# Top-k attention with two MLPs on one core: spreading each block's MLP work past the next block's start

## The chip, the core and the metric

One core of one Trainium2 chip runs the whole program in one launch. The core has five engines that run side by side, each through its own list of instructions in order: PE (TensorE, matrix products and transposes), DVE (VectorE), ACT (ScalarE), POOL (GpSimd) and SP (SyncE, which only issues DMAs). They wait for each other through semaphores. The metric is the device time of the launch in microseconds (us); a change of about half a per cent is what a measurement of this kernel can tell from none.

## The reference

```
scores = q @ k.T / sqrt(64)          # 4 batches, 8 heads, 576 tokens
kth    = 32nd largest of each row
attn   = softmax over the scores that are >= kth, the others count as nothing
x      = attn @ v                    # put together to 2304 tokens x 512
h      = relu(x @ w_in);   x = (h * h) @ w_out        # first MLP, 512 -> 2048 -> 512
h      = x @ w2_in; x = max(0.01 h, h) @ w2_out       # second MLP, same sizes
```

The weights come as float64, all else as float32.

## The kernel before

The attention is cut into tiles of 128 score rows, two tiles to a pair, 72 pairs in all. A pair's scores come from PE (L303, evacuated by ACT at L304), its 32 largest values from 8 MAX8 and 6 MATCH_REPLACE8 on DVE (L867, L869), its softmax from ACT (L321, L325) and POOL, then PE transposes it (L339 for the first 512 columns, 8 instructions for a pair, L354 for the last 64) and multiplies it with v (L425 for the first two units, L436 from then on). Every fp32 value on the fast matmul path is split into a high and a low part.

The table `UNITS` gives the order in which (batch, first token, tokens) go through the attention: units of 256, 256, 256, 64, 320, 256, 256, 320 and 320 tokens, each over four head pairs. The finished tokens are collected in that order in six blocks of 512, 256, 384, 512, 256 and 384 (`BLOCKS`). When a block is full, its MLP work can start: layer 0 and layer 1, each in 16 steps of 128 hidden rows (the function `moe`). A step is 12 matmuls for the hidden rows (L619) and 6 to 12 for the accumulation (L656 in layer 0, L658 in layer 1); ACT and POOL (DVE in the last block) make the activation between them (L629 to L639). `moe` is a generator that gives up control after every three matmuls; such a portion is called a quantum below.

Block 0 is special: its 32 steps are the first to use the weights, so 32 times 1 MB of float64 is loaded (L511, `wraw`), turned into high and low parts by ACT, DVE and POOL (L532 to L553, `wc`, `wi`, `wo`) and stored to DRAM (L566, L567) for the later blocks, which load the parts back (L574, L575).

A block's x lies in one of three buffer sets (`SETS` = 0, 1, 0, 1, 0, 2), so block 2 writes where block 0 was, and block 3 where block 1 was. The end of each unit and head pair is `x_out`, which writes x into the block that is being filled.

The order of the program is written by a loop over slots at the end of the function, 16 slots for a pair, one DVE instruction in 14 of them. In each slot, events (scores, transposes, v products, loads) are emitted with a higher priority, and then `run_moe` emits as many quanta as the current rate has earned. The rate of a block was fixed ahead: its quanta over the slots until the next block is full, less one (`rate`). When the next block is full, whatever is left of the one before is emitted at once. From this, a scheduler with a priority for each instruction makes the final list of each engine; attention is put ahead where its inputs are thought to be ready, and MLP matmuls fill in.

By those slots blocks 0 to 5 are full about when the transposes of pairs 16, 24, 36, 52 and 62 and the end of the attention are reached.

The unit of 64 tokens is `KEPT`: its scores are made early, beside batch 0's others, parked in DRAM and loaded back when its turn comes. `HI_SET` (0 to 15) lists which unit-and-head-pair numbers have the high part of q and v made by ACT; for the others POOL makes it.

Of the kernel before, what the change touches and what calls it, by code (L numbers as in the profile page):

```python
# [24 lines left out]


UNITS = [
    (0, 0, 256), (0, 256, 256), (1, 0, 256), (0, 512, 64), (1, 256, 320),
    (2, 0, 256), (3, 0, 256), (2, 256, 320), (3, 256, 320),
]  # L30

# [6 lines left out]
SETS = (0, 1, 0, 1, 0, 2)  # L38
# [5 lines left out]

NATIVE = 2

KEPT = 3

EARLY = (2, 3)
FILL = (2, 245)  # L50
# [13 lines left out]
LEAD = 24  # L64

SOON = 100
SEAM = 400
CONVP = 30

# [17 lines left out]
def topk_attention_moe_moe2_kernel(  # L87
# [97 lines left out]
    for i in range(4):  # L185
        x = const if i < 2 else ahead
# [206 lines left out]
    blocks = []  # L393
# [78 lines left out]
    def unspill(blk):  # L472
        m = blk["spilled"]
        for c, (xh, xl) in enumerate(block_x(blk)):
            split_hi(xh[:, 0:m], spill[:, c, 0:m])
            POOL.tensor_tensor(xl[:, 0:m], spill[:, c, 0:m], xh.bitcast(F)[:, 0:m], op=OP.subtract)
# [201 lines left out]
    def quanta(j, layer):  # L678
        return NF * (NK + (NK if layer == 0 else blocks[j]["n"] // P))
# [121 lines left out]
    for uh in uhs:  # L801
# [16 lines left out]
        if uh["u"]["i"] == NATIVE - 1 and uh["hp"] == NHP - 1:  # L818
            at(z, open_late)
        rmark(uh, z)  # L820
    rate = []
    for j, blk in enumerate(blocks):
        nxt = rslot[j + 1] if j + 1 < len(blocks) else rslot[j] + 40
        rate.append(sum(quanta(*ph) for ph in groups[j]) / max(nxt - rslot[j] - 1, 40))

    def convert_now(i):
        for _ in w_convert(i):
            pass
# [12 lines left out]
    def run_moe(amount):  # L841
        while amount >= 1 and active:
            try:
                next(active[0])
                amount -= 1
            except StopIteration:
                active.pop(0)
        return amount
# [3 lines left out]
    while slot <= last:  # L852
        p, i = divmod(slot, 16)
        if slot >= 0 and p < NPAIRS:
            pr = pairs[p]
            if i == 0:
                pr["m8"] = pool.tile([P, 2, 32], F, tag="m8", name="m8", bufs=2)
                pr["sum"] = pool.tile([P, 2], F, tag="sum", name="sum", bufs=2)
                pr["rc"] = pool.tile([P, 2], F, tag="rc", name="rc", bufs=2)
                for t in pr["t"]:  # L860
                    t["w"] = pool.tile([P, S], F, tag="w", name="w", bufs=2)
            x = i % 2
            t = pr["t"][x]
            m8 = pr["m8"]
            r = i // 4
            if i < 14 and i % 4 < 2:
                cur["dve"] = DVE.max(out=m8[:, x, 8 * r:8 * r + 8], in_=t["s"] if r == 0 else t["w"])  # L867
            elif i < 14:
                cur["dve"] = DVE.match_replace(out=t["w"], in_to_replace=m8[:, x, 8 * r:8 * r + 8],  # L869
                                               in_values=t["s"] if r == 0 else t["w"], imm_value=NEG)  # L870
        if slot == rslot[0]:
            open_mlp()
        for fn, a in events.pop(slot, []):
            nr = len(ready)
            with tc.high_priority(offset=SOON):
                fn(*a)
            for blk in ready[nr:]:
                if not (len(ready) > nr + 1 and blk is ready[-1]):
                    while active:
                        run_moe(1)  # L880
                if blk["idx"] + 1 < len(blocks) and blocks[blk["idx"] + 1].get("spilled"):
                    unspill(blocks[blk["idx"] + 1])
                active.extend(moe(*ph) for ph in groups[blk["idx"]])
                credit = 0.0
                cur["rate"] = rate[blk["idx"]]
        if active:
            credit = run_moe(credit + cur["rate"])
        slot += 1
# [54 lines left out]
```

## Time and profile before

| | us |
|---|---|
| median of the three runs shown (1189.94, 1193.88, 1194.23) | 1193.88 |
| the profiled execution's own time | 1189.77 |
| its span, first to last instruction | 1188.0 |
| PE busy | 1124.0 (95%) |
| DVE busy | 872.1 (73%) |

The rows further down come from the profiled execution. A window row gives the busy time of each engine in a stretch of the span. In the timeline a row merges equal instructions that follow each other; its second number runs to the modelled end of the last one, which overlaps the next row, so the pace of matmuls is read from start to start. An entry in square brackets is idle time just before the row, with what ended it. The chain of waits follows the last instruction of a stretch back to what released each step.

### The profile page before, as it was taken

What the parts mean: (1) busy time and instruction counts of PE and PEld (TensorE: products, weight loads), DVE (VectorE), ACT (ScalarE), POOL (GpSimd) and SP (SyncE); (2) the same over time, 40 slices, a digit from 0 to 9 for tenths busy, and PEclk for the clock granted to TensorE, in tenths of its full rate; (3) what the DMA queues carried; (4) which work ended last, traced back from release to release, by engine and by line L of the source; (5) the groups of instructions that cost most, each with busy time, mean ns of one, the idle gap of its engine ahead of it and who ended that gap; (6) DMA issues with size and microseconds to landing.
All of it is one profiled execution on the core that took longest, in us unless ns stands there. A gap on an engine that the chain in (4) does not pass through costs nothing.

```text
span 1188.0 us, 20096 instructions
## 1 busy us (share of the span) xinstructions
PE 1124.0 (95%) x6376; PEld 985.5 (83%) x6376; DVE 872.1 (73%) x1828; ACT 820.1 (69%) x1823; POOL 744.8 (63%) x958
## 2 busy tenths in 40 slices
PE   5899977989899999999999999999999999999997
PEld 4777765868688899898998998788888899998996
DVE  7999999888886668999999999989997400110010
ACT  6999998899989667887676777556766743332322
POOL 7968846999879677677886775767665653002100
PEclk9999989999899999999999999999999999999999
DMA  9868756899999698799888888667776499779973
GB/s 307 287 216 276 264 187 230 312 334 333 394 353 360 199 336 293 240 346 371 312 264 296 286 283 287 217 219 219 232 234 215 151 326 334 256 252 351 346 258 119
DMA packets 108201, 329.53 MB, mean 277 GB/s; under 512 B 17216, under 2 KB 25408, under 8 KB 104000
## 3 DMA queue, kind: packets, MB, share of 16 engines
q1 hardware_dynamic: 105472, 323.53, 79.8%
q10 hardware_dynamic: 2624, 4.72, 1.1%
q8 instruction: 52, 0.85, 0.3%
q14 instruction: 53, 0.43, 0.1%
HBM read 257.03 MB, written 71.17 MB: 276 GB/s over the span
## 4 chain that ended last, share of the span: by engine, by line
PE 57%; DVE 21%; ACT 12%; DMA 5%; issue 2%; POOL 2%; ACTq 0%; SPq 0%; POOLq 0%; DVEq 0%
PE h L619 22%; PE acc L658 13%; DVE m L867 10%; PE acc L656 9%; DVE w L869 8%; PE att L425 3%; PE att L436 3%; PE att L339 3%; ACT e L321 2%; ACT stage L304 1%; PE sp L303 1%; ACT e L325 1%; DMA wraw<-in_w_dram 1%; DMA out_dram<-y 1%; ACT s L304 1%
## 5 line engine op out<-in xcount | busy, mean ns | idle before, releaser
L619 PE MATMUL h<-xh,wi 128*128 128x512 f32 (+2 forms) x1280 | 345.9, 344 | 9.7 <-ACT ga L629 4.5
L867 DVE MAX8 m<-w 128x8 f32<-128x576 f32 x432 | 315.1, 756 | 1.8
L619 PEld LDWEIGHTS h<-xh,wi 128*128 128x128 f32 x1280 | 225.4, 190 | 38.6 <-ACT ga L629 6.7
L639 POOL TENSOR_TENSOR gl<-ga,gh 128x512 fp32r<-128x512 f32 (+2 forms) x160 | 162.5, 1018 | 137.2 <-ACT gh L638 110.9
L869 DVE MATCH_REPLACE8 w<-m,w 128x576 f32<-128x576 f32 x288 | 215.2, 751 | 0.5
L619 PE MATMUL h<-xl,wi 128*128 128x512 f32 (+2 forms) x640 | 203.3, 338 | 0.0
L347 POOL TENSOR_TENSOR PTs<-whole,PTs 128x512 fp32r<-128x512 f32 x112 | 144.6, 1297 | 43.7 <-ACT whole L346 43.2
L656 PE MATMUL acc<-gh,wo 128*128 128x512 f32 (+2 forms) x768 | 156.5, 343 | 0.8 <-ACT y L674 0.5
L658 PE MATMUL acc<-wo,gh 128*128 128x512 f32 x576 | 152.1, 396 | 0.5 <-ACT gh L638 0.5
L656 PEld LDWEIGHTS acc<-gh,wo 128*128 128x128 f32 x768 | 127.4, 190 | 13.4 <-ACT y L674 0.7
L321 ACT ACTIVATE e<-s,m 128x576 f32<-128x576 f32 x144 | 112.9, 785 | 32.3 <-DVE m L867 27.4
L639 DVE TENSOR_TENSOR gl<-ga,gh 128x384 fp32r<-128x384 f32 x32 | 17.9, 559 | 152.1 <-ACT gh L638 149.4
L619 PEld LDWEIGHTS h<-xl,wi 128*128 128x128 f32 x640 | 120.0, 189 | 10.6
L636 ACT ACTIVATE ga<-h 128x512 f32<-128x512 f32 (+2 forms) x96 | 46.6, 491 | 116.3 <-PE h L619 114.8
L658 PEld LDWEIGHTS acc<-wo,gh 128*128 128x128 f32 x576 | 105.4, 188 | 21.2 <-ACT gh L638 0.9
L867 DVE MAX8 m<-s 128x8 f32<-128x576 f32 x144 | 104.3, 754 | 17.7 <-ACT s L304 15.2
L325 ACT ACTIVATE e<-e,nb 128x576 f32<-128x576 f32 x144 | 111.5, 782 | 1.8 <-POOL nb L315 1.7
L869 DVE MATCH_REPLACE8 w<-m,s 128x576 f32<-128x576 f32 x144 | 108.2, 752 | 0.6
L339 PE MATMUL att<-ident,e 128*128 128x128 f32 x576 | 90.1, 277 | 7.6 <-DVE wc L548 3.0
L334 POOL TENSOR_SCALAR e<-e,rc 128x576 f32<-128x576 f32 x112 | 82.5, 748 | 16.0 <-DVE rc L330 14.5
L656 PE MATMUL acc<-gl,wo 128*128 128x512 f32 (+2 forms) x384 | 88.3, 349 | 3.8 <-POOL gl L639 3.8
L631 POOL TENSOR_TENSOR ga<-ga 128x512 f32<-128x512 f32 (+2 forms) x80 | 66.3, 829 | 36.9 <-ACT gh L630 36.7
(90 smaller groups left out, 2117.4 us busy)
## 6 DMA issues: line engine op xcount, KB each, us to landing
wi<-wd SPq DMA_DIRECT2D x160, 512.0 KB, 5.1
wo<-wd SPq DMA_DIRECT2D x160, 512.0 KB, 5.0
wraw<-in_w_dram SPq DMA_DIRECT2D x32, 1024.0 KB, 7.9
sd<-stage SPq DMA_DIRECT2D x76, 288.0 KB, 3.3
s<-sd SPq DMA_DIRECT2D x76, 288.0 KB, 4.8
wd<-wi SPq DMA_DIRECT2D x32, 512.0 KB, 7.8
wd<-wo SPq DMA_DIRECT2D x32, 512.0 KB, 8.4
vd<-VT SPq DMA_DIRECT2D x16, 640.0 KB, 5.8
```

The source lines that it names most:

```text
L321: ACT.activation(t["e"], t["s"], AF.Prelu, bias=pr["m8"][:, i, 31:32], scale=-1.0, alpha=1.0 / FAR)
L325: ACT.activation(e, e, AF.Exp, bias=pr["nb"][:, i:i + 1], scale=-FAR, accum_out=pr["sum"][:, i:i + 1])
L334: POOL.tensor_scalar(e, e, pr["rc"][:, i:i + 1], 1.0, op0=OP.mult, op1=OP.mult)
L339: PE.transpose(ps[:, j * P:(j + 1) * P], t["e"][:, j * P:(j + 1) * P], ident)
L347: POOL.tensor_tensor(pts[:, 4:8, c:c + P], whole, pts.bitcast(F)[:, 0:4, c:c + P], op=OP.subtract)
L619: PE.matmul(two[r][:, 0:n], lhsT=ws[r][:, w, c * P:(c + 1) * P], rhs=x[c][y][:, 0:n], start=cnt == mine[0], stop=cnt == mine[-1])
L631: POOL.tensor_tensor(a[:, 0:n], a[:, 0:n], a[:, 0:n], op=OP.mult)
L639: (DVE if j >= GLD else POOL).tensor_tensor(gl[:, 0:n], a[:, 0:n], gh.bitcast(F)[:, 0:n], op=OP.subtract)
L656: PE.matmul(acc[c][:, 0:n], lhsT=wo[:, w, cs], rhs=g[:, 0:n], start=first, stop=last)
L658: PE.matmul(acc[c], lhsT=g[:, cs], rhs=wo[:, w, :], start=first, stop=last)
L867: cur["dve"] = DVE.max(out=m8[:, x, 8 * r:8 * r + 8], in_=t["s"] if r == 0 else t["w"])
L869: cur["dve"] = DVE.match_replace(out=t["w"], in_to_replace=m8[:, x, 8 * r:8 * r + 8], in_values=t["s"] if r == 0 else t["w"], imm_value=NEG)
```

## The change

Four things change.

1. A block's quanta are no longer emitted at once when the next block is full. They stay in front of the list, and the next block's are put behind them. The rate is set when a block is full: all quanta then open, over the slots until the next block is full plus 24 (`LATE`). Block 0's rate goes from 256 quanta over 127 slots to 256 over 152.
2. Before an `x_out` opens a new block, everything still open of a block in the same buffer set is emitted.
3. In `UNITS` the 64 tokens of batch 0 go behind the 320 of batch 1, both still in block 2, so that the first `x_out` of block 2 comes after 320 tokens' first head pair and not after 64 tokens'. `KEPT` follows.
4. `HI_SET` is not touched, but its numbers 12 to 15 now mean the head pairs of the unit of 320: their q goes to ACT, and the q and v of the 64 tokens to POOL.

```diff
--- before.py
+++ after.py
@@ -25,7 +25,7 @@
 
 
 UNITS = [
-    (0, 0, 256), (0, 256, 256), (1, 0, 256), (0, 512, 64), (1, 256, 320),
+    (0, 0, 256), (0, 256, 256), (1, 0, 256), (1, 256, 320), (0, 512, 64),
     (2, 0, 256), (3, 0, 256), (2, 256, 320), (3, 256, 320),
 ]
 
@@ -44,7 +44,7 @@
 
 NATIVE = 2
 
-KEPT = 3
+KEPT = 4
 
 EARLY = (2, 3)
 FILL = (2, 245)
@@ -64,6 +64,7 @@
 LEAD = 24
 
 SOON = 100
+LATE = 24
 SEAM = 400
 CONVP = 30
 
@@ -818,11 +819,6 @@
         if uh["u"]["i"] == NATIVE - 1 and uh["hp"] == NHP - 1:
             at(z, open_late)
         rmark(uh, z)
-    rate = []
-    for j, blk in enumerate(blocks):
-        nxt = rslot[j + 1] if j + 1 < len(blocks) else rslot[j] + 40
-        rate.append(sum(quanta(*ph) for ph in groups[j]) / max(nxt - rslot[j] - 1, 40))
-
     def convert_now(i):
         for _ in w_convert(i):
             pass
@@ -841,7 +837,8 @@
     def run_moe(amount):
         while amount >= 1 and active:
             try:
-                next(active[0])
+                next(active[0][0])
+                active[0][1] = max(active[0][1] - 1, 0)
                 amount -= 1
             except StopIteration:
                 active.pop(0)
@@ -872,17 +869,19 @@
             open_mlp()
         for fn, a in events.pop(slot, []):
             nr = len(ready)
+            if fn is x_out and "x" not in blocks[cur["fill"]]:
+                shared = [x for x in range(cur["fill"]) if SETS[x] == SETS[cur["fill"]]]
+                while any(x[2] in shared for x in active):
+                    run_moe(1)
             with tc.high_priority(offset=SOON):
                 fn(*a)
             for blk in ready[nr:]:
-                if not (len(ready) > nr + 1 and blk is ready[-1]):
-                    while active:
-                        run_moe(1)
-                if blk["idx"] + 1 < len(blocks) and blocks[blk["idx"] + 1].get("spilled"):
-                    unspill(blocks[blk["idx"] + 1])
-                active.extend(moe(*ph) for ph in groups[blk["idx"]])
-                credit = 0.0
-                cur["rate"] = rate[blk["idx"]]
+                j = blk["idx"]
+                if j + 1 < len(blocks) and blocks[j + 1].get("spilled"):
+                    unspill(blocks[j + 1])
+                active.extend([moe(*ph), quanta(*ph), ph[0]] for ph in groups[j])
+                todo = sum(x[1] for x in active)
+                cur["rate"] = todo / (rslot[j + 1] - slot + LATE if j + 1 < len(blocks) else 40)
         if active:
             credit = run_moe(credit + cur["rate"])
         slot += 1
```

What this does to PE's list is shown at three places. The number of matmuls of every kind is the same before and after. Line numbers above 66 are one higher in the changed kernel up to the loop (L340 is L339 before, L620 is L619).

The first place is PE's list where block 0 goes from layer 0 to layer 1: `acc` from `gl` and `gh` ends layer 0, `h` from `xh` and `xl` opens layer 1, `att` from `ident` and `e` are the transposes of a pair, `att` from `KT` and `q` are scores. Before:

```order
L656 MATMUL acc<-gh,wo 128x512 x8
L303 MATMUL att<-KT,q_83 128x288
L303 MATMUL att<-KT,q_84 128x288
L339 MATMUL att<-ident,e_107 128x128 x4
L339 MATMUL att<-ident,e_108 128x128 x4
L303 MATMUL att<-KT,q_83 128x288
L303 MATMUL att<-KT,q_84 128x288
L303 MATMUL att<-KT,q_83 128x288
L303 MATMUL att<-KT,q_84 128x288
L656 MATMUL acc<-gl,wo 128x512 x4
L619 MATMUL h<-xh_649,wi 128x512 x4
```

After:

```order
L355 MATMUL att<-ident,e_107 64x128
L355 MATMUL att<-ident,e_108 64x128
L437 MATMUL att<-PTs,VT 128x256 x9
L657 MATMUL acc<-gl,wo 128x512 x4
L657 MATMUL acc<-gh,wo 128x512 x8
L657 MATMUL acc<-gl,wo 128x512 x4
L304 MATMUL att<-KT,q_77 128x288
L304 MATMUL att<-KT,q_78 128x288
L304 MATMUL att<-KT,q_77 128x288
L304 MATMUL att<-KT,q_78 128x288
L620 MATMUL h<-xh_649,wi 128x512 x8
L620 MATMUL h<-xl_650,wi 128x512 x2
```

The eight transposes that stood ahead of the last `gl` accumulation now stand some 30 MLP matmuls earlier, in front of the piece shown; four score matmuls that also stood ahead of it have come behind it.

The second place is PE's list where block 1 begins (`h` of 256 columns is block 1, `acc` from `wo` is still block 0's layer 1). Before:

```order
L339 MATMUL att<-ident,e_107 128x128 x4
L658 MATMUL acc<-wo,gh 128x512 x2
L658 MATMUL acc<-wo,gl 128x512 x4
L619 MATMUL h<-xh_3222,wi 128x256 x4
L619 MATMUL h<-xl_3223,wi 128x256
L658 MATMUL acc<-wo,gh 128x512 x8
L619 MATMUL h<-xh_3222,wi 128x256 x2
L339 MATMUL att<-ident,e_108 128x128
L303 MATMUL att<-KT,q_77 128x288
L339 MATMUL att<-ident,e_108 128x128
L303 MATMUL att<-KT,q_78 128x288
```

After:

```order
L659 MATMUL acc<-wo,gh 128x512
L304 MATMUL att<-KT,q_83 128x288
L304 MATMUL att<-KT,q_84 128x288
L659 MATMUL acc<-wo,gl 128x512 x4
L355 MATMUL att<-ident,e_109 64x128
L355 MATMUL att<-ident,e_110 64x128
L437 MATMUL att<-PTs,VT 128x320
L620 MATMUL h<-xh_3152,wi 128x256 x4
L620 MATMUL h<-xl_3153,wi 128x256
L620 MATMUL h<-xh_3152,wi 128x256 x2
L620 MATMUL h<-xl_3153,wi 128x256
```

Both lists mix the end of block 0 with the opening of block 1. Before, this stands at the transposes of pair 24 (the first and the last rows shown); now it stands behind those of pair 25, with the products with v of the unit of 320 tokens between.

The third place is PE's list at the transposes of pairs 47 and 48 (`h` of 384 columns is block 2, layer 1). Before, from the products with v ahead of pair 48's transposes on:

```order
L619 MATMUL h<-xh_5191,wi 128x384 x4
L658 MATMUL acc<-wo,gh 128x512 x2
L436 MATMUL att<-PTs,VT 128x256 x7
L339 MATMUL att<-ident,e_107 128x128 x2
L436 MATMUL att<-PTs,VT 128x256
L339 MATMUL att<-ident,e_107 128x128 x2
L339 MATMUL att<-ident,e_108 128x128 x4
L658 MATMUL acc<-wo,gh 128x512 x4
L658 MATMUL acc<-wo,gl 128x512 x3
```

After, from pair 47's transposes to pair 48's:

```order
L340 MATMUL att<-ident,e_109 128x128 x4
L340 MATMUL att<-ident,e_110 128x128 x4
L620 MATMUL h<-xl_5297,wi 128x384 x2
L355 MATMUL att<-ident,e_109 64x128
L355 MATMUL att<-ident,e_110 64x128
L437 MATMUL att<-PTs,VT 128x256
L340 MATMUL att<-ident,e_107 128x128 x4
```

Before, 41 MLP matmuls stand between the first transposes of pairs 47 and 48; now there are two.

Counted over the whole list, the MLP matmuls that stand ahead of the first transposes of pair 28, 53 and 71 were 1052, 2184 and 2940, and are 911, 2067 and 2796.

## Rows read from the trace of the kernel before

**Rows 1.** The page, busy time of each engine: time, share, instructions.
```profile
PE 1124.0 (95%) x6376; PEld 985.5 (83%) x6376; DVE 872.1 (73%) x1828; ACT 820.1 (69%) x1823; POOL 744.8 (63%) x958
```

**Rows 2.** Windows: PE, PEld, DVE, ACT, POOL busy, clock, DMA, GB/s.
```profile
178.00:320.00 142.00, 125.64 (x562) 98.38 (x562) 125.63 (x241) 127.69 (x246) 122.59 (x128) 0.95 0.89 316
320.00:450.00 130.00, 129.45 (x747) 112.58 (x748) 91.20 (x181) 101.29 (x207) 97.59 (x109) 1.00 0.89 320
450.00:750.00 300.00, 291.17 (x1836) 270.00 (x1835) 295.68 (x641) 222.96 (x499) 225.08 (x298) 1.00 0.86 294
750.00:950.00 200.00, 199.61 (x990) 166.14 (x989) 167.46 (x362) 132.42 (x276) 130.43 (x157) 1.00 0.66 214
950.00:1188.00 238.00, 229.98 (x1419) 217.66 (x1417) 23.06 (x44) 76.94 (x170) 37.81 (x53) 0.99 0.81 280
```

**Rows 3.** Chain of waits by line: 178:320, 320:450, 450:740.
```profile
by line: DMA wraw<-in_w_dram 11.8%; ACT att L541 7.2%; issue 6.4%; DVE m L867 5.9%; ACT wc L532 5.7%; DVE w L869 5.4%; PE h L619 5.2%; DVE wc L547 5.1%; DVE wc L548 4.4%; PE acc L656 3.9%; ACT wo L552 3.8%; DMA vraw<-in_v_dram 3.7%; PE att 
...
by line: PE h L619 37.3%; PE acc L658 33.7%; PE att L436 6.9%; PE acc L656 6.6%; DMA out_dram<-y 5.5%; PE att L339 3.6%; PE att L303 3.1%; ACT y L674 1.3%; PE att L354 0.7%; ACT s L304 0.4%; ACT PTs L344 0.4%; ACT whole L346 0.4%; issue 0.1
...
by line: DVE m L867 36.3%; DVE w L869 26.8%; PE acc L658 5.6%; PE h L619 5.6%; issue 3.4%; DVE PTs L364 3.0%; DVE xf L442 2.4%; PE att L436 1.8%; ACT e L321 1.6%; DMA out_dram<-y 1.6%; ACT e L325 1.6%; PE att L303 1.5%; ACT PTs L344 1.4%; A
```

**Rows 4.** Timeline of the PE: first transposes of pairs 16, 28, 53 and 71.
```profile
193.18 0.27 PE L339 MATMUL att<-ident,e 128*128 128x128 f32 x1
...
466.51 0.38 PE L339 MATMUL att<-ident,e 128*128 128x128 f32 x2
...
733.76 0.49 PE L339 MATMUL att<-ident,e 128*128 128x128 f32 x3
...
951.27 0.49 PE L339 MATMUL att<-ident,e 128*128 128x128 f32 x3
```

**Rows 5.** Timeline of the PE: back-to-back runs, and the row behind each.
```profile
332.34 2.03 PE L658 MATMUL acc<-wo,gh 128*128 128x512 f32 x8
334.21 0.39 PE L658 MATMUL acc<-wo,gl 128*128 128x512 f32 x1
...
432.94 1.11 PE L656 MATMUL acc<-gh,wo 128*128 128x256 f32 x8
433.90 0.64 PE L656 MATMUL acc<-gl,wo 128*128 128x256 f32 x4
434.37 0.42 PE L303 MATMUL att<-KT,q 128*128 128x288 f32 x2
434.64 0.41 PE L354 MATMUL att<-ident,e 128*64 128x128 f32 x2
...
437.49 1.87 PE L436 MATMUL att<-PTs,VT 128*128 128x64 f32 x16
439.20 0.36 PE L619 MATMUL h<-xh,wi 128*128 128x256 f32 x1
...
694.46 0.33 PE L619 MATMUL h<-xh,wi 128*128 128x384 f32 x1
694.63 0.34 PE L619 MATMUL h<-xl,wi 128*128 128x384 f32 x1
```

**Rows 6.** Windows from pair 16 to pair 28; columns as in rows 2.
```profile
193.00:304.00 111.00, 101.29 (x466) 81.13 (x464) 95.34 (x183) 101.17 (x192) 104.58 (x107) 0.97 0.92 323
304.00:466.00 162.00, 157.04 (x922) 137.01 (x923) 121.92 (x239) 130.47 (x271) 123.58 (x140) 0.98 0.90 324
```

**Rows 7.** Timeline of the PE: its waits where block 0 changes layers.
```profile
304.30 0.66 PE L339 MATMUL att<-ident,e 128*128 128x128 f32 x4 [1.77 <-ACT s L304]
306.53 1.08 PE L339 MATMUL att<-ident,e 128*128 128x128 f32 x4 [1.58 <-DVE wc L548]
```

**Rows 8.** Timeline of the PE: its waits where block 3 begins.
```profile
736.59 0.50 PE L619 MATMUL h<-xh,wi 128*128 128x512 f32 x1 [1.58 <-ACT ga L629]
743.91 1.20 PE L656 MATMUL acc<-gl,wo 128*128 128x512 f32 x4 [1.06 <-POOL gl L639]
```

**Rows 9.** Groups by line, DVE, 320 to 450: count, busy, mean, idle before.
```profile
L547 DVE SCALAR_TENSOR_TENSOR wc<-att,wc 128x512 uint32<-128x512 uint32 x23 | 15.1, 682 | 6.2 <-ACT wc L532 3.8 <-ACT att L541 2.4
```

## The prediction

> **What bounds the kernel now.** I read the page first: PE is busy 95% of the span, DVE 73%, ACT 69%, POOL 63% [rows 1]. That is a mean over unlike stretches, so the windows come next, cut where the busy shares change [rows 2], and beside each the chain of waits [rows 3].
>
> - 178 to 320, the first half of block 0's MLP, with the weight conversion: nobody is full for good. PE has 125.6 of 142 us, ACT 127.7, POOL 122.6, DVE 125.6, and the chain is a mix of weight loads, ACT conversions and DVE. The granted clock averages 0.95: some 14 us at 1.2 GHz.
> - 320 to 450, block 0's second half and the start of block 1: PE has 129.5 of 130 us and the chain is PE's matmuls. DVE is idle for 38.8 us, because the attention comes up late in PE's list.
> - 450 to 750: DVE has 295.7 of 300 us, and MAX8 and MATCH_REPLACE8 are 63% of the chain. PE is at 291.2.
> - 750 to 950: PE again, 199.6 of 200. DVE has 32.5 us idle.
> - From 950 on only MLP work is left, and PE has all of it.
>
> So PE sets the end, except between 450 and 750. The change adds no matmul and takes none away; what it can earn is PE's idle time. Idle after pair 16 begins: about 10 and 5 us between pairs 16 and 28 [rows 6], then 9 us in the DVE stretch [rows 2], and next to nothing in 750 to 950.
>
> **The change part by part.** I divide PE's list at the first transposes of pairs 16, 28, 53 and 71, which started at 193.2, 466.5, 733.8 and 951.3 [rows 4]. The stretches took 273.3, 267.2, 217.5 us, and 236.7 to the end of the span at 1188.0. Prices per matmul come from start-to-start times of unbroken runs [rows 5]: 512 columns (334.21 - 332.34)/8 = 0.23; 384 columns 0.17; 256 columns (433.90 - 432.94)/8 = 0.12; 64 columns (439.20 - 437.49)/16 = 0.107; scores (434.64 - 434.37)/2 = 0.135. Products with v of 320 columns I put at 0.14, between the 256 and 384 columns.
>
> From the two lists, kind by kind:
> - Pair 16 to 28: 141 MLP matmuls of 256 columns fewer (-16.9), the 72 products of the 64 tokens gone (-7.7), 2 of 512 (+0.5), 20 scores and 18 products of 320 tokens more (+5.2). Sum -18.9 us.
> - Pair 28 to 53: those 141 and 72 come in (+24.6), the scores and products go out (-5.2), 48 of 384 (-8.2) and 69 of 512 columns (-15.9) fewer. Sum -4.7 us.
> - Pair 53 to 71: 48 of 384 more (+8.2), 63 of 512 (-14.5) and 12 of 256 (-1.4) fewer. Sum -7.7 us.
> - From pair 71 on: 132 of 512 and 12 of 256 columns more, +31.8 us.
>
> That adds up to nothing, as it must. But a stretch that DVE sets does not get shorter when PE's work in it does. Pair 28 to 53 is 25 pairs at 267.2/25 = 10.7 us, DVE's pace, so its -4.7 us are not earned: **+4.7**. In 53 to 71 DVE would need 18 x 10.7 = 193 us, under PE's 217.5 - 7.7, so PE's saving counts there.
>
> PE's idle time from pair 16 to 28. The work of ACT and POOL to the end of layer 0 is almost what it was: PE's list shows 28 fewer MLP matmuls ahead of pair 20's transposes (352, before 380), so layer 0 ends only half a pair later. What moves is the wait at its end. The transposes that waited 1.8 and 1.6 us there [rows 7] had score matmuls and the last accumulation behind them, and the slow clock followed. In the new list the transposes stand some 30 matmuls, or 7 us, further forward; PE comes to them sooner by about the 28 matmuls (6.4 us) it has not yet done, and ACT and DVE are not sooner by as much. Between 0 (the wait moves along) and -7 (3.4 us of waits and half of one slow spell, of which the 14 us hold two), I take -4: ACT, which is what was waited for, loses the activations of those 28 matmuls, two steps of four or five operations.
>
> Block changes. Where block 3 begins, PE waited 1.6 and 1.1 us for the first activations of the new block [rows 8], because nothing of block 2 was left. Now block 2's last 45 or so matmuls stand beside the attention there. That is worth -2.6; bounds 0 and -4.
>
> Lumps. In the new list the MLP matmuls per pair are uneven from pair 34 on: 60, 74 and 72, then 36 and 18; 72 at pair 44, 2 at pair 48 and 61 at 49. PE has about 49 us of work from pair 40 to 44, by the prices above, where DVE needs 42.8; then 29 from 44 to 48. If PE is late with scores, DVE stalls, and in this stretch DVE is the bound. DVE runs two to three pairs ahead, which covers most of it. Bounds 0 and +12 (6.6 here and about as much at pairs 34 to 36), I take +3. The empty place at pair 48 costs nothing by itself while DVE sets the pace.
>
> The moved q and v splits: 8 of ACT's small operations go to POOL, behind pair 32, where POOL is busy 225 of 300 us [rows 2]. Nothing waits for a POOL with 25% spare; if its cover failed, 8 x 0.5 us would come on top. The new rule before `x_out` never has to emit anything: block 0's last quantum comes by slot 426, and the first `x_out` of block 2 at slot 450; with the 64 tokens in front it would have been 418. Weight loads and stores are as many as before, in the same order.
>
> Sum: 4.7 - 4 - 2.6 + 3 = +1.1. Against the profiled execution's own 1189.77 us that is 1190.9. That execution lies 4.1 below the median of the runs shown, which spread from 1189.9 to 1194.2; I forecast the middle of that, **1192 us**, no change.
>
> Two rules of the Trainium skill bear on this. The page Perfetto Trace Analysis, section Optimization Strategy, says that a kernel whose most contended engine changes over time can gain by interleaving its regimes. The trace has such regimes, DVE 70% busy from 320 to 450 and 99% from 450 to 750 [rows 2]; by that rule the change goes the right way, and the first rival below is what it would bring. The page TensorE: Matmul & The Clock Gate, Part 1, says that the array falls to half clock after it has been idle. The trace agrees with 0.95 granted from 178 to 320, where PE waited; by that rule the empty place at pair 48 could cost a slow spell, which the sum leaves out since 450 to 750 was granted 1.00 all through.
>
> **The rivals.**
>
> *The late attention is pulled forward (faster).* If PE meets the transposes of pairs 21 to 28 as early as its list now allows, DVE's 38.8 us of idle from 320 to 450 shrink to about 5, 34 us earned; 7.7 from pair 53 on; against 31.8 more behind pair 71. With the 2.6 at block 3 that is -12, **1178 us** from 1189.8. For it: PE does 130 us without a gap when it is fed [rows 2]. Against: in the 125 us or so before, PE, ACT and POOL are all near 90%, so the attention cannot be made much faster there.
>
> *PE waits for the attention from pair 24 to 28 (slower).* The new list has 60 and 40 MLP matmuls ahead of pairs 25 and 26 where it had 103 and 95. In DVE's new list pairs 24 to 26 have 41 bit operations of the conversion among them, at 15.1/23 = 0.66 us [rows 9]: 27 us beside three pairs at 10.7, 59 in all. PE's work from pair 24 to 27 is 39 us by the prices, so 20 are missing, and only DVE's lead can pay for them. Before, the same three pairs had 47 such operations, 63 us for DVE against 46 of PE work by the prices, PE hardly waited [rows 2], and the lead paid for the 17. If it pays 17 again, 3 are lost; if nothing, 20. In the middle 12: **1203 us**. It decides when PE reaches pair 25: with DVE two pairs or more ahead it costs little, with one pair it is all there. For it: the conversions' waits on ACT and on the weight loads lead the chain [rows 3]. Against: ACT, at 231.6 us of 273 from pair 16 to 28 [rows 6], has 15% to spare.
>
> *The scheduler undoes it.* The matmuls that leave pairs 16 to 28 are only 19 us of 273, and the list had been uneven already from pair 53 on; then both waits stay where they are and the time is that of before, the same class as the forecast.
>
> **How the numbers follow.** No change, with the case in which the scheduler undoes it, 0.40; faster 0.31; slower 0.29. About half a per cent (6 us) is what a measurement of this kernel can tell from no change, so faster means under 1188 and slower over 1200. The forecast's own range is 1184 to 1199: the bounds of its terms, -8 to 0, -4 to 0 and 0 to +12 around +4.7, rarely all at one end. For 8 in 10 it has to reach past both rivals: 1175 to 1207, the lower end with the better bound of the wait at block 0's seam, the upper with a slow spell of the clock on top of 1203.
>
> **What would show it.** In the new profile PE should reach pair 28's first transposes near 444 (466.5 - 18.9 - 4), pair 53's near 714 (25 pairs at 10.7, and 3), and pair 71's near 921, with 268 us behind it. DVE should be at 99% over some 270 us, and idle less from 320 to 450. The waits of 1.6 and 1.1 us at block 3's start should be gone. A pair 28 later than 452 speaks for the slower rival, one before 438 for the faster. The forecast is wrong if pair 28 to 53 is not DVE's stretch any more, or if PE's idle time before pair 28 changes by more than 8 us.

## The result, and the profile after

The changed kernel took 1204.09 us (median of 4 runs, 1202.45 to 1207.22), the kernel before 1192.68 us in the same job: a ratio of 1.0101, with a 95% interval of 1.0071 to 1.0131. It is slower by 1%, where 1192 and "no change" were forecast. The profiled execution took 1207.22 us, with a span of 1205.1 at a mean granted clock of 0.985 (before 1188.0 at 0.988).

The page's first row, which answers to [rows 1], shows next to nothing, as it must where the same work is only ordered anew. DVE's 872.1 us have become 875.5:

```profile
PE 1130.1 (94%) x6376; PEld 989.9 (82%) x6376; DVE 875.5 (73%) x1828; ACT 819.6 (68%) x1815; POOL 746.2 (62%) x966
```

The PE timeline of the changed kernel at the first transposes of pairs 16, 28, 53 and 71 is the answer to [rows 4] (start, us, engine, line, operation):

```profile
198.49 0.41 PE L340 MATMUL att<-ident,e 128*128 128x128 f32 x1
...
457.74 0.38 PE L340 MATMUL att<-ident,e 128*128 128x128 f32 x2
...
724.66 0.38 PE L340 MATMUL att<-ident,e 128*128 128x128 f32 x2
...
932.59 0.27 PE L340 MATMUL att<-ident,e 128*128 128x128 f32 x1
```

And its windows between these marks, with 320 to 450 behind them for comparison with [rows 2] (columns as there):

```profile
198.50:457.70 259.20, 240.04 (x1217) 198.26 (x1216) 219.46 (x417) 226.62 (x449) 209.19 (x215) 0.98 0.86 300
457.70:724.70 267.00, 257.11 (x1694) 243.09 (x1693) 263.95 (x576) 196.98 (x446) 213.06 (x292) 0.99 0.91 315
724.70:932.60 207.90, 206.30 (x1038) 173.17 (x1037) 183.14 (x398) 142.21 (x296) 141.58 (x171) 1.00 0.70 225
932.60:1205.10 272.50, 262.42 (x1553) 243.22 (x1550) 22.66 (x43) 83.22 (x179) 43.07 (x56) 0.99 0.78 266
...
320.00:450.00 130.00, 124.69 (x658) 104.45 (x658) 105.99 (x199) 110.73 (x222) 92.32 (x95) 1.00 0.83 287
```

PE reaches pair 71 18.7 us earlier (932.6, before 951.3), and DVE's idle time from 320 to 450 fell from 38.8 to 24.0 us. But behind pair 71 there are 272.5 us in place of 236.7, 35.8 more. The two together are the 17.1 us between the two spans, which is more than the 11.4 us between the medians: the profiled execution of the changed kernel was the slowest of its four. One profile can lie some us off, so both kernels were profiled again (e12 to e14). Means of two profiles of before and three of after, in us, beside the forecast's terms:

```
stretch          before  after   moved   PE work by the list   forecast
start to 16      194.8   197.6    +3.0           -0.5             none
16 to 28         273.0   257.1   -15.9          -18.9         -18.9 - 4
28 to 53         267.3   267.1    -0.3           -4.7     -4.7 + 4.7 + 3
53 to 71         217.9   207.9   -10.0           -7.7          -7.7 - 2.6
behind 71        236.2   272.8   +36.6          +31.8            +31.8
sum                              +13.4              0             +1.1
```

The four work terms of the prediction add up to +0.5 us, which it put at nothing. The rest of the list has the other -0.5: 22 MLP matmuls stand ahead of pair 16, before 24.

### The profile page after: what moved, and what is told of

Its sections match the earlier page's. It is cut to its first block, busy times and chain, and to the rows that moved or that the text cites. A ratio compares the mean times of both kernels' runs of the same rounds, so it can differ in the third digit from the quotient of the medians.

```text
span 1205.1 us, 20102 instructions
## 1 busy us (share of the span) xinstructions
PE 1130.1 (94%) x6376; PEld 989.9 (82%) x6376; DVE 875.5 (73%) x1828; ACT 819.6 (68%) x1815; POOL 746.2 (62%) x966
## 4 chain that ended last, share of the span: by engine, by line
PE 63%; ACT 11%; DVE 10%; DMA 7%; POOL 4%; issue 3%; ACTq 0%; POOLq 0%; DVEq 0%
PE h L620 25%; PE acc L657 13%; PE acc L659 12%; DVE m L864 4%; DMA wraw<-in_w_dram 4%; PE att L437 4%; DVE w L866 3%; PE att L340 3%; PE att L426 2%; ACT stage L305 1%; PE sp L304 1%; ACT e L326 1%; DMA out_dram<-y 1%; ACT s L305 1%; ACT att L542 1%
## 5 line engine op out<-in xcount | busy, mean ns | idle before, releaser
L620 PE MATMUL h<-xh,wi 128*128 128x512 f32 (+2 forms) x1280 | 348.3, 346 | 11.0 <-ACT ga L637 2.9
L620 PEld LDWEIGHTS h<-xh,wi 128*128 128x128 f32 x1280 | 226.4, 190 | 38.2 <-ACT ga L637 4.8
L620 PE MATMUL h<-xl,wi 128*128 128x512 f32 (+2 forms) x640 | 206.4, 341 | 0.0
L620 PEld LDWEIGHTS h<-xl,wi 128*128 128x128 f32 x640 | 121.1, 191 | 10.7 <-issue 0.3
L864 DVE MAX8 m<-s 128x8 f32<-128x576 f32 x144 | 104.0, 750 | 18.6 <-ACT s L305 15.3
L340 PE MATMUL att<-ident,e 128*128 128x128 f32 x576 | 88.7, 278 | 7.3 <-ACT whole L347 2.3
L345 ACT ACTIVATE PTs<-att 128x512 fp32r<-128x512 f32 x112 | 67.0, 598 | 36.9 <-PE att L340 36.1
```

What stands on the lines that cost most here:

```text
L340: PE.transpose(ps[:, j * P:(j + 1) * P], t["e"][:, j * P:(j + 1) * P], ident)
L345: ACT.activation(pts[:, 0:4, c:c + P], x, AF.Copy)
L620: PE.matmul(two[r][:, 0:n], lhsT=ws[r][:, w, c * P:(c + 1) * P], rhs=x[c][y][:, 0:n], start=cnt == mine[0], stop=cnt == mine[-1])
```

## The experiments

Three theories stood at first. A: the sum by stretches is right, only PE's idle time in the front was mis-sized. B: the 64 tokens' products and their v split on POOL, now among pairs 28 to 53, are what costs. C: the spreading by 24 slots is. Later ones are D (work that leaves the attention's part comes back behind it at full price, and the attention earns it only down to DVE's pace), E (the list before is a lucky one, any other costs 12 to 20 us), and F, which is D with a seam that falls behind pair 71. One table serves all runs: MLP matmuls that stand ahead of pair 71, each stretch of the run's own profile with the PE work of its list in parentheses (matmuls by kind, at the paces of [rows 5]), and the median time. The kernel before, measured beside each group of these runs, had medians from 1190.0 to 1193.1 us, so two runs are compared by their ratios to it:

```
run                   ahead  to 16  16 to 28     28 to 53     53 to 71     behind 71     median
before (2 profiles)   2940   194.8  273.0 (248)  267.3 (253)  217.9 (211)  236.2 (226)   1192.7
after (3 profiles)    2796   197.6  257.1 (229)  267.1 (248)  207.9 (203)  272.8 (258)   1204.1
e1 swap only          2796   196.9  260.8 (236)  266.7 (245)  206.4 (199)  272.1 (258)   1207.3
e2 spread only        2796   196.0  268.9 (231)  269.2 (258)  201.6 (191)  272.8 (258)   1206.1
e3 LATE = 0           2820   195.4  266.0 (238)  266.8 (243)  212.5 (204)  265.8 (252)   1212.8
e4 splits on ACT      2772   196.4  259.0 (227)  268.4 (250)  202.8 (197)  278.8 (264)   1208.9
e5 spread late only   2868   194.4  272.4 (248)  267.4 (253)  203.1 (195)  256.3 (241)   1197.4
e6 block 0 by 8       2892   197.0  274.1 (242)  266.4 (259)  209.2 (201)  247.0 (236)   1193.7
e7 after, copy to DVE 2844   199.5  258.4 (232)  271.7 (257)  209.9 (202)  260.0 (247)   1200.8
e8 before, the same   2868   196.9  279.3 (248)  271.2 (248)  203.9 (200)  255.5 (241)   1208.0
e9 after, less ACT    2796   198.5  255.4 (229)  266.7 (248)  209.2 (203)  272.7 (258)   1203.7
e10 after, less DVE   2796   194.9  249.8 (224)  269.8 (248)  214.1 (209)  272.6 (258)   1203.1
e11 before, DVE to POOL 2892 194.4  278.1 (248)  266.1 (253)  204.9 (201)  246.4 (236)   1189.1
e15 block 0 as before 2844   197.4  260.2 (236)  268.8 (247)  214.3 (208)  261.3 (247)   1205.4
e16 after, DVE to POOL 2724  198.9  258.5 (229)  255.2 (227)  212.3 (207)  288.1 (275)   1214.8
```

**e1, e2: each half of the change alone.**

```diff
 e1: before, and only  -  (1, 0, 256), (0, 512, 64), (1, 256, 320)   KEPT = 3
                       +  (1, 0, 256), (1, 256, 320), (0, 512, 64)   KEPT = 4
 e2: after, with these two lines as they were
```

> The kernel before with the 64 tokens behind the 320 (UNITS, KEPT) and nothing else; rate and emptying as before. Theory A (the sum by stretches, with the PE idle times that the changed kernel showed: 28 us from pair 16 to 28, 267 us by DVE from 28 to 53, then PE): its list has 236, 245, 199 us of PE work and 258 behind pair 71, so 1199 us, half of the loss. Theory B (the moved 64 tokens are the cost, with their v split by POOL inside the DVE stretch): 1204, all of the loss. Theory C (the spreading is the cost): 1193, none.

> The changed kernel with the 64 tokens in front of the 320 again; the spreading, the run-on and the emptying before x_out stay. Its list has 230, 258, 191 us of PE work and 258 behind pair 71. Theory A: 1193 to 1196. Theory B (the 64 tokens): 1193, as before. Theory C (the spreading): 1204, as the changed kernel.

Ratios to before: 1.0144 [1.0118, 1.0170] and 1.0135 [1.0107, 1.0164]. Each half costs as much as both. Where one part alone were to blame, the other would have been free: B and C both fall. Both put the same 2796 MLP matmuls ahead of pair 71. A was 8 us low for e1 and 10 to 13 for e2. In e2's profile, which is of its slowest run (1210.27 us), the front (pairs 16 to 28) earned 4 us of 17:

```profile
196.00:464.90 268.90, 248.70 (x1247) 206.47 (x1246) 213.19 (x413) 224.59 (x446) 219.21 (x232) 0.95 0.86 305
```

The granted clock is 0.95 there, 0.98 in the changed kernel and 0.98 and 0.97 in the two profiles of before. At 0.95 some 13 us of clock are missing in this stretch, at 0.98 some 5; that is 5 to 8 more than in the two profiles of before, beside 13 us that were not earned. Where the rest went, and whether the slow clock cost its full price, is not shown.

**e3, e4: two numbers of the changed kernel.**

```diff
 e3: -LATE = 24                        +LATE = 0
 e4: -HI_SET = (0, ..., 11, 12, 13, 14, 15)   +HI_SET = (0, ..., 11, 16, 17, 18, 19)
```

> The changed kernel with LATE = 0: the run-on without the 24 more slots. PE work 238, 243, 204 and 252 behind pair 71. Theory A: 1200. Theory B: 1204, since the 64 tokens stay behind. Theory C: 1195, near the kernel before with only the run-on left.

> The changed kernel with the high parts of the 64 tokens' q and v on ACT again and the 320's q on POOL (HI_SET 0 to 11 and 16 to 19). In the changed kernel's trace PE waited 1.9, 1.0 and 0.5 us for POOL at 501 to 511 us, where POOL splits that v. Theory A: PE work 227, 250, 197 and 264 behind pair 71, about 1203. Theory B: 1200, the waits at 501 to 511 gone and 4 us back. Theory C: 1204, no change.

1.0182 [1.0157, 1.0207] and 1.0167 [1.0139, 1.0195]. No theory's figure was met: e3 came 9 to 18 us above the three, e4 5 to 9. Taking the spreading's 24 slots away does not give the time back, nor does the split of the 64 tokens on ACT. e3's own profile, of its fastest run, adds up to 1206.6 and its median lies higher; why is open, and it is slower than the changed kernel with less work behind pair 71.

**e5, e6, e15: the spreading in some blocks only.**

```diff
 e5:  before's units; LATE by block (-1, 24, 24, 24, 24), and the list emptied when block 1 is ready
 e6:  before's units; LATE by block (8, -1, -1, -1, -1), and emptied when blocks 2 to 5 are ready
 e15: after;          LATE by block (-1, 24, 24, 24, 24), and emptied when block 1 is ready
```

> The kernel before, with the spreading by 24 slots from the second block on only (old order of the left tokens, block 0 as before). Its matmul list is that of the kernel before through pair 53 (2184 MLP matmuls ahead of it); between pairs 53 and 71 there is 195 us of PE work in place of 211, behind pair 71 241 in place of 226. Theory D (what leaves the attention's part comes back behind it at full price, and the attention's part only shortens down to DVE's pace of 10.7 us a pair): the first three marks as before, 53 to 71 200 to 204 us in place of 217.5, the tail 252 to 254 in place of 236.7: 1190 to 1196. Theory E (the list of before is a lucky one, and any other costs 12 to 20 us wherever it differs): 1202 to 1210.

> The kernel before, with block 0 alone spread over 8 more slots (old order of the left tokens, later blocks as before). PE work 241.9 / 258.8 / 200.9 / 235.7 us in the four stretches (before 247.5 / 253.1 / 210.7 / 226.0). Theory D: 16 to 28 earns only a part of its 5.6 (270 us), 28 to 53 stays 270, 53 to 71 208, tail 247: 1188 to 1194. Theory E: 1202 to 1210.

> The changed kernel with block 0 not spread (its list emptied when block 1 becomes ready, as before), the 24 slots from block 1 on and the new order of the left tokens kept: 2844 MLP matmuls ahead of pair 71 in place of 2796, PE work 236 / 247 / 208 / 247 us. Theory F (the price is what falls behind pair 71, plus a seam or two that lie uncovered there, and the stretch 28 to 53 held at 267 by DVE): pair 16 at 197, 16 to 28 261, 28 to 53 267, 53 to 71 212, behind it 260: span 1197, median 1195 to 1201. If the new order of the left tokens is what costs (1207 with the swap alone), it stays at 1203 to 1208.

Measured 1.0053 [1.0037, 1.0069], 1.0020 [1.0011, 1.0030] and 1.0117 [1.0097, 1.0136]. E falls as a rule for any list: both lists of e5 and e6 differ from before's and cost 6 and 2.5 us. e6 is in D's range; e5 is 1.4 above it. e5 shows the price of the tail by itself, since all of PE's list up to pair 53 is before's: 53 to 71 shortened by 14.8 us for 15.3 of work, and the part behind 71 grew by 20.1. Of the last 5 us, 3 are time in which PE is not busy, at a seam (below). PE is busy for 245.3 of 256.3 us behind pair 71 in e5, and for 228.7 of 236.7 in the kernel before:

```profile
937.34:1193.68 256.34, 245.29 (x1481) 229.48 (x1479) 23.07 (x44) 79.92 (x174) 39.17 (x53) 0.99 0.79 270
...
951.27:1187.98 236.71, 228.71 (x1409) 216.39 (x1407) 23.06 (x44) 76.29 (x168) 36.62 (x51) 0.99 0.81 281
```

e15 was 4 us over F's range and lies in the range set for the case that the new order of the left tokens is what costs. Its stretches came out at 260, 269, 214 and 261, forecast 261, 267, 212 and 260: small misses, all but one of one sign. In the new order block 0's spreading carries no cost (e15 costs as much as the changed kernel). In the old order it does: e2 and e5, which differ in how block 0 is emitted, cost 1.35% and 0.53%. So the costs of the parts do not add up, and no single part carries them. The swapped order alone (e1) takes 8 us of work out of 28 to 53, which stays as long as it was.

**e7, e8: ACT's 24 plain copies of pairs 16 to 27 onto DVE, in after and in before.**

```diff
-            ACT.activation(whole, x, AF.Copy)
+            if 32 <= t["i"] < 56:
+                DVE.tensor_scalar(whole, x, 1.0, 1.0, op0=OP.mult, op1=OP.mult)
+            else:
+                ACT.activation(whole, x, AF.Copy)
```

> The changed kernel, with the plain copy of a P-tile (whole, 604 ns on ACT, 24 of them) moved from ACT to DVE for pairs 16 to 27, that is 14.5 us less of ACT in the stretch in which PE waits for it. The scheduler then puts 2844 MLP matmuls ahead of pair 71 in place of 2796. Theory D with ACT as what holds the front: pair 16 to 28 falls from 259 to about 252 with 3 us more PE work in it, the tail from 272 to 261, together 1189 to 1195. If ACT is not what holds it (DVE, or PE's own order): 16 to 28 stays near 262, 1197 to 1204. Theory E: 1202 to 1210.

> Control: the same move of 24 copies from ACT to DVE in the kernel before. Its list keeps 1052 MLP matmuls ahead of pair 28 and has 2868 in place of 2940 ahead of pair 71. Theory D with ACT: PE's waits for ACT there are 7 us in place of 14, so 16 to 28 gains less, 273 to 268; 28 to 53 268; 53 to 71 207; tail 252: 1186 to 1192. If ACT is not what holds it: 1190 to 1196. Theory E: 1202 to 1210.

1.0084 [1.0069, 1.0098] and 1.0151 [1.0132, 1.0170]. e7 is in the range for "not ACT". The front of the changed kernel did not get shorter (258.4 with 3 us more PE work in it, mean 257.1), so its better time is the tail's: 48 more matmuls stand ahead of pair 71. e8 is 12 us above the highest figure of D and inside E's range, and no theory here explains it. In the kernel before, the front got 6 us longer, though PE's list there kept its counts and DVE was busy for only 229 of the 279 us. The stretch 28 to 53 went to 271 and 272; in e8 DVE carried some 4 us of work into it, in e7 it was idle for 5 us more, and why is open.

**e9, e10: less ACT, less DVE in the front of the changed kernel.**

```diff
 e9:  -ACT.activation(whole, x, AF.Copy)                            for pairs 16 to 27; POOL takes pts in its place
 e10: -DVE.scalar_tensor_tensor(bx, vu, 0x80000000, bx, ...)        L549, 64 times
```

> The changed kernel without the plain copies of the P-tiles of pairs 16 to 27 (24 x 604 ns of ACT; the low halves of these P-tiles come out as zero, that part of the computation is left out; nothing is moved to another engine). Its matmul list has the changed kernel's counts (910, 2067 and 2796 MLP matmuls ahead of pairs 28, 53, 71; PE work 229 / 248 / 203 / 258 us). If ACT is what PE waits for between pairs 16 and 28 (14 us of recorded waits, 7 in the kernel before): that stretch falls from 259 to 249 to 253, the rest stays, 1194 to 1199. If not ACT (DVE, transfers, or chains through several engines that a shorter ACT queue doesn't shorten): 257 to 260, 1201 to 1206.

> The changed kernel without the second of the two DVE operations on each half of a weight block (L549, 64 x 0.68 us, nearly all between pairs 14 and 28; the weights lose their sign bits, that part of the computation is left out). Its list has 5 us less PE work between pairs 16 and 28 (224), 209 in place of 203 between 53 and 71, the same behind 71. If DVE's work holds PE between pairs 16 and 28: the stretch falls by 15 or more (244 or less), 1190 to 1196. If not: it falls by no more than the 5 us of work, to 254, 1200 to 1208.

1.0106 [1.0085, 1.0127] and 1.0101 [1.0081, 1.0121]. Both times are in the ranges for "if not". e9's front is within the three profiles of the changed kernel (255.4 to 259.2): ACT's copies are not what holds it, though PE's waits there name ACT for 14 of 21 us. e10's fell by 7.3 us, between the two cases of its expectation; 5.1 of them are PE work, and 32 us less of DVE, as its window from pair 16 to 28 shows, bought 2:

```profile
194.90:444.70 249.80, 236.86 (x1169) 196.14 (x1168) 187.45 (x361) 224.77 (x446) 207.90 (x213) 0.97 0.87 304
```

Neither engine alone holds the front. A third candidate was not tested, the weight loads. The chain of waits from pair 16 to 28 has them (`wraw`) at 6.1% in the kernel before and at 18.2% in the changed one:

```profile
by line: PE h L619 19.6%; PE acc L658 16.0%; DMA wraw<-in_w_dram 6.1%; PE acc L656 5.6%; DVE m L867 4.8%; DVE w L869 4.3%; issue 3.4%; ACT att L541 3.4%; PE att L436 3.3%; ACT wc L532 3.0%; DVE wc L547 2.7%; DMA out_dram<-y 2.6%; DVE wc L54
...
by line: DMA wraw<-in_w_dram 18.2%; PE h L620 12.8%; PE acc L657 7.5%; issue 6.5%; PE acc L659 5.1%; DVE w L866 3.9%; ACT att L542 3.9%; DVE m L864 3.8%; DVE wc L548 3.5%; DVE wc L549 2.9%; ACT wc L533 2.7%; PE att L437 2.3%; DMA out_dram<-
```

The other profiles have 3.3% before (e14) and 20.3 and 11.1% after (e12, e13).

**e11, e16: DVE's subtraction L364 (L365) for pairs 28 to 52 onto POOL, behind an ACT copy, in before and in after.**

```diff
-                DVE.tensor_tensor(pts[64:128, 8, c:c + m], ps[0:64, o:o + m], ...)
+                if 56 <= pr["t"][0]["i"] < 106:
+                    ...
+                    ACT.activation(l, ps[0:64, o:o + m], AF.Copy)
+                    POOL.tensor_tensor(pts[64:128, 8, c:c + m], l, ...)
```

> The kernel before, with DVE's subtraction of the last 64 keys' P-tile (L364, 27 x 398 ns between pairs 28 and 53) taken to POOL behind a plain ACT copy, for pairs 28 to 52. The list is that of before up to pair 53, and has 2892 in place of 2940 MLP matmuls ahead of pair 71 (201 us of PE work between 53 and 71 in place of 211, 236 behind in place of 226). If 28 to 53 is DVE's stretch: it falls from 267 to 258 to 262 (PE has 253 us of work in it), 53 to 71 205 to 208, the tail 247 to 250: 1179 to 1187, faster than both kernels. If PE or its order holds the stretch: 267, 1190 to 1194.

> The changed kernel with DVE's subtraction of the last 64 keys' P-tile (some 27 x 398 ns, 10.7 us in all) taken to POOL behind a plain ACT copy for pairs 28 to 52. The scheduler then leaves only 227 us of PE work between pairs 28 and 53 (248 in the changed kernel, 253 in the kernel before), 207 between 53 and 71 and 275 behind 71. If DVE holds 28 to 53 whatever PE's list has there: the stretch falls by the 10.7 us of DVE to 255 to 258, and the other 10 us of PE's relief are lost: 211 between 53 and 71, 288 to 290 behind, 1210 to 1216. If PE's list holds it: it falls by 21 to 246, 1200 to 1206.

e16 tells it: 10.7 us of DVE gone, and the stretch fell by 11.9, where PE's work fell by 21. PE is idle for 16 of the 255 us, DVE for 2:

```profile
457.30:712.50 255.20, 239.01 (x1588) 223.85 (x1587) 253.01 (x548) 194.13 (x461) 225.35 (x313) 0.99 0.89 308
```

The time was 1214.84 us in one run (1210 to 1216 expected). In e11 the same stretch stayed at 266.1, since PE has 261.1 us busy there in the kernel before:

```profile
466.50:733.80 267.30, 261.11 (x1636) 242.52 (x1635) 264.68 (x576) 198.36 (x443) 199.67 (x266) 1.00 0.87 298
```

Before, both engines are close to full from 28 to 53 (PE busy for 261 and DVE for 265 of 267 us); after, DVE is (264) and PE has 257. So e11's first expectation, on the stretch, fell. Still it has the lowest median of all: 1189.13 us (12 runs), 0.9971 [0.9958, 0.9985] of before, though 0.3% is less than the half per cent named at the start. Its profiled execution, the slowest of the twelve, does not show where from: 13 us less between 53 and 71, 10 more behind it, and 5 more in the front, of which 4 are the delay told of in the last section.

**e12, e13, e14: more profiles of after (two) and before.** The kernels are as they were.

> The changed kernel again, for a second profile. If the 5 us before pair 16 and the 4.8 us that the stretch from pair 16 to 28 fails to earn belong to the changed list, they stand here too (pair 16 at 198 to 199, 16 to 28 258 to 261). If they are single delays of one execution, either is 3 us or more off.

> The changed kernel again, for a third profile, with the same two expectations.

> The kernel before again. Two kernels with its list through pair 28 had 272.4 and 278.1 us for the stretch from pair 16 to 28 (273.3 in its own profile), so a second profile should give 193 to 195 for pair 16 and 271 to 278 for the stretch.

Single runs of 1202.12, 1204.38 and 1192.21 us. Pair 16 at 197.1, 197.2 and 196.4; 16 to 28 took 255.4, 256.7 and 272.6. Both of the changed kernel came about 1 us sooner to pair 16 and 1 to 3 us sooner through the front than the ranges for a lasting delay, and the kernel before came to pair 16 1.4 us later than its range. So of the 5.3 and 4.8 us that the first profile of the changed kernel showed there, about 3 each belong to its list.

## Why the prediction was wrong

The prediction's cut of the list held: the matmul counts, and the stretch that DVE sets. The total failed by 12 us, by these steps, largest first.

- **PE's idle time from pair 16 to 28, the wait at block 0's layer change (-4): failed, the stretch lost 3 more in place of 4 less.** Pair 28 was reached at 452.5 to 457.7 in the three profiles, where 444 was forecast. "PE comes to them sooner ... and ACT and DVE are not sooner by as much" weighed a gain that was not there. The two waits of [rows 7] stand in the changed kernel at the same seam, as long as before:

```profile
310.59 0.41 PE L355 MATMUL att<-ident,e 128*64 128x128 f32 x2 [1.99 <-ACT s L305]
312.51 0.86 PE L437 MATMUL att<-PTs,VT 128*128 128x256 f32 x4 [1.51 <-DVE wc L549]
```

 Only a third wait of 1.0 us, which stood behind them before, is gone. That is close to the bound 0 of the term, "the wait moves along". The rest is scattered: over its own work PE lost, in the means, 0.1 us more than before between pairs 16 and 20, 1.3 more between 20 and 24 and 1.7 more between 24 and 28. No list tried here came under 24 us for the three together (25.5 before, 28.5 after). What sets that floor stays open; e9 and e10 show that it is neither ACT's copies nor DVE alone.
- **Behind pair 71 (+31.8, measured +36.6): too small by 4.8.** The list had the work right, but the forecast priced it at the matmuls' pace alone. In the windows between the marks PE is busy for 34.0 us more (228.7 and 228.1 before, 262.4, 262.1 and 262.7 after) and not busy for 2.6 more. Part of the 2.6 are two waits. The first, at the end of block 3, is for the read-out of its accumulators (`y`), which now falls where no attention stands beside it; it is new behind pair 71. The second, for the new x of block 5, stood there before too, with 0.58 us (third row):

```profile
975.84 0.50 PE L657 MATMUL acc<-gh,wo 128*128 128x256 f32 x2 [1.29 <-ACT y L675]
...
1020.16 1.51 PE L620 MATMUL h<-x,wi 128*128 128x384 f32 x7 [0.90 <-DVE xl L672]
...
1002.15 1.15 PE L619 MATMUL h<-x,wi 128*128 128x384 f32 x5 [0.58 <-DVE xl L671]
```

 And the windows of the changed kernel around its two, in which PE misses 2.8 us of 40:

```profile
972.00:992.00 20.00, 18.20 (x146) 17.56 (x147) 0.00 (x0) 5.95 (x15) 8.65 (x14) 1.00 0.98 337
1012.00:1032.00 20.00, 19.04 (x120) 18.63 (x120) 3.09 (x7) 8.19 (x19) 2.70 (x4) 1.00 0.89 307
```

 The table bears it out as a step: what lies behind pair 71 takes 10 to 11 us over its work in the lists with up to 236 us of it (before, e6, e11), and 13 to 15 in all with 241 or more. Why PE's busy time grew by 34.0 us and not by 31.8 is open but for 0.5: 1.87/8 is 0.234, and the prediction took 0.23 for each of the 132 matmuls of 512 columns.
- **Start to pair 16 (no term in the sum, measured +3.0 with 0.5 less work): left out.** The prediction put it at nothing without a reason; PE's list there hardly changes. Five profiles have the list of before up to there (before, e5, e8, e11, e14: 193.2 to 196.9 us) and five that of the changed kernel (after, e9, e12, e13, e16: 197.1 to 198.9). DVE is nearly full there too: idle for 8.9 and 10.8 us of it in the two profiles of before, 11.3 to 12.2 in the three of the changed kernel. e10, with 5 operations of the conversion ahead of pair 16 in place of 11 or 12, reaches it at 194.9, 2.7 us sooner. The granted clock of the stretch goes with it, 0.96 or 0.97 in the first five and 0.93 to 0.95 in the others:

```profile
0.00:193.18 193.18, 161.11 (x885) 129.70 (x886) 184.23 (x396) 170.25 (x455) 137.13 (x225) 0.97 0.76 251
...
0.00:198.49 198.49, 164.17 (x882) 132.14 (x883) 186.26 (x398) 170.58 (x447) 139.34 (x234) 0.95 0.75 245
```

 Which of DVE's waits grew was not told apart, nor whether the clock is a cause or follows from PE's waits.
- **Lumps (+3): cost nothing.** 28 to 53 took 267.1, and DVE was idle in it for 3.0 us, before 2.6. The +3 that was taken for them made up for as much of the other errors, by luck.
- **DVE's stretch, "not earned" (+4.7): right.** With 243 to 259 us of PE work it took 266 to 270 us in all runs but e7, e8 (271 to 272) and e16; taking 10.7 us from DVE took it to 255 (e16, one run).
- **Block 3's seam (-2.6): right.** 53 to 71 shortened by 2.3 more than its work, and the waits of [rows 8] are gone. Where block 3 begins in the changed kernel, PE's row has no idle time before it:

```profile
746.10 1.08 PE L620 MATMUL h<-xh,wi 128*128 128x512 f32 x4
```

Summed: 7 + 4.8 + 3.5 - 3.3 + 0.3 is the 12.3 us between the forecast's +1.1 and the +13.4 measured (3.5 because the list has 0.5 us less work ahead of pair 16).

Over the work of the list the changed kernel so lost 3.5 us ahead of pair 16, 3.0 in the front, 4.4 in DVE's stretch and 4.8 behind pair 71, and gained 2.3 between 53 and 71. DVE's stretch is shown by e16, and the size of the tail's loss by the table; the 6.5 us ahead of pair 28 have no cause that a run shows.

Of the rivals, the slower one (1203) was near in time, and pair 28 came later than 452 as it asked, but not by its mechanism: PE lost 1.7 us more between pairs 24 and 28, not 12. So its nearness is luck. The faster one fell: DVE's idle time from 320 to 450 did shrink, but by 15 of the 34 us it counted on, and the 23.3 us by which pair 71 came sooner (in the means) are less than the 36.6 behind it. The Trainium skill's page Perfetto Trace Analysis, section Optimization Strategy, says that interleaving regimes may gain. It did not here: pair 71 came sooner, and the time grew by 1%. The kernel before empties a block's list when the next block is ready, so spreading a block can only push work back.

## What to carry to other kernels

Where a change only reorders a full engine's list, cut the list at the points where another engine is the bound, and count what leaves a stretch that the other engine sets as lost. Then look at where that work comes back: a seam that lay beside other work can cost more where nothing stands beside it. And profile the same kernel twice before a difference of some us in one stretch is explained.

## What the runs showed of the hardware

e11 and the kernel before have the same instructions in the same order on PE, ACT, DVE and POOL up to pair 28, and yet 16 to 28 took 278.1 us in the one and 273.3 and 272.6 in two profiles of the other. Most of it comes from one place: in e11 PE waited there for an ACT copy, at a place where the kernel before did not wait (434.37 in [rows 5]):

```profile
438.07 0.53 PE L303 MATMUL att<-KT,q 128*128 128x288 f32 x2 [1.91 <-ACT whole L346]
439.05 0.41 PE L354 MATMUL att<-ident,e 128*64 128x128 f32 x2 [0.44 <-ACT whole L346]
```

The granted clock fell behind it; windows of e11 around the place:

```profile
435.00:440.00 5.00, 2.65 (x17) 2.08 (x17) 2.04 (x4) 3.78 (x10) 3.23 (x4) 0.94 1.02 395
440.00:445.00 5.00, 5.00 (x35) 5.00 (x34) 4.50 (x12) 4.15 (x12) 4.16 (x7) 0.72 0.98 328
```

From 440 to 445 the clock averages 0.72 (1.2 GHz for part of it, 2.4 for the rest), and 4.2 us were lost in all. The Trainium skill's page TensorE: Matmul & The Clock Gate, Part 1, says that the array drops to half clock after it has been idle. This trace agrees: the clock fell behind waits of 1.91 and 0.44 us, and it stayed at 1.00 from 430 to 440 in the kernel before, where PE was busy all through. In a kernel that is full, one wait of 2 us cost twice its length, and with the same instructions it fell in one of three profiles.
